# A kernel's work written as named jobs in one list, and its PSUM handed out as four pairs of banks from one queue

## The chip, the core and the metric

The kernel runs on one core of a Trainium2 chip. A core has a matrix engine (TensorE, PE in the profile, with its weight loads shown apart as PEld), a vector engine (VectorE, DVE), an engine for activations and copies (ScalarE, ACT), a general engine (GpSimd, POOL), and a queue engine that issues DMA transfers (SyncE, SP). Each runs its own instructions in program order and waits on semaphores for the others. Matmul results go to PSUM, which the kernel uses as eight banks of 512 fp32 numbers per partition; ScalarE or VectorE must copy a result out ("evict" it) before its banks can be written again.

The metric is the device time in microseconds. Before the change it is 213.2 us, the median of three runs (213.05 to 213.38).

## The reference

Two independent computations on sequences of length S = 2048 and width D = 576 in bf16, whose results stand side by side in the output.

```python
# A: 32 heads of width 18; every position attends to 8 positions at distance 0, 2, ..., 14
qkv = (x @ wqkv) -> q, k, v
logits = einsum("bhsd,bhswd->bhsw", q, kg) * scale     # kg: k at s - 2w, masked below 0
attn = softmax(logits)
a = einsum("bhsw,bhswd->bhsd", attn, vg) @ wo
# B: a 4-tap filter over k, times v, then a long convolution by FFT
k_shift = sum over t of k_pad[:, t:t+S] * shift_k[:, 3-t]
kv = k_shift * v
y = irfft(rfft(kv, 2S) * rfft(ssm_k, 2S))[:S] + kv * ssm_D
b = q * y
out = concatenate([a, b], -1)
```

## The kernel before

**Part A.** `project` makes q, k and v: for each block of 128 output columns and half of the sequence, a `unit` of eight to ten 512-wide matmuls fills a pair of banks (L363, L367, and the rest of the contraction in `tails`, L374, L380), and ScalarE evicts 1024 columns (L397). `logits` multiplies q by shifted k on VectorE (`product`, L822, into one of two halves of the tile `av`, or, for every third one while v's space there is still unused, into the tile `v`), and `total` sums over the head's columns with matmuls (L837) into one pair per five products; ScalarE evicts to `av` (L842). `softmax` runs on VectorE (L865 to L869, L882) and ScalarE (L871, L878, L879), with the sum over the eight positions on TensorE (L877). `spread` copies weights by DMA, `weigh` multiplies by v on VectorE (L947) and sums on TensorE (L964, L978), and `output` is the last projection (L1012, L1020), evicted by ScalarE (L1031).

**Part B.** `taps` computes kv in four blocks on VectorE (L560, L564, L580). `mirror` folds a block with matmuls into two pairs (L589, evicted by L592). `fold_filter` does the same with a block of the long filter (L650 into two pairs, L653), followed by three accumulating DMAs from POOL (L655, L657, L658). `filter_spectrum` transforms the filter (L610 and L611, evicted by L670), `x_spectrum` transforms kv (L766, L768). VectorE multiplies the spectra (L1098), TensorE adds the products (`sum_of`, L1126, two pairs held for a group, evicted by L1139), `inverse` transforms back (L1158, L1177, evicted by L1161, L1179; L1185 and L1199, evicted by L1206) and VectorE multiplies by q (L1212, L1167) before the store.

**What sets the order.** The scheduling of the framework is off (`manual_schedule`): instructions run in the order in which the Python code emits them. TensorE's fill-in work is collected as tuples in the list `units`; `until` emits the next few at each step of the main line, as many as the tuple `PLACES` says, and `need(label)` emits until none with that label is left. Further tuples (`FKS`, `FXS`, `EARLY`, `AT`) place single kinds, and a small model of the engines' clocks (`clk`, `pe`, `dve`) decides which unit comes first in some places and when late work (`tasks`) is due.

**PSUM.** The pool `pp` has two tags, "A" and "B", with two buffers each; every buffer is a pair of banks:

```python
pp = ctx.enter_context(tc.tile_pool(name="pp", bufs=2, space=PSUM))
def bank2(name, tag):
    return pp.tile([128, 2, 512], FP32, name=name, tag=tag)
```

A new tile of a tag takes the buffer of the tile two before it on that tag, and its first matmul waits until that one has been read. "A" serves projections, the filter folds (`ps_rev`, two at once), tables, outputs and the inverse; "B" serves the first transposes, mirrors (two at once), logits, softmax sums, weighted sums and the sums of products (two held). Filter and kv spectra alternate by `filler_tag`: filter units take "A" alone until the logits begin and then A, A, B in turn, kv units A and B.

Of the kernel before, what the change touches and what calls it, by code (L numbers as in the profile page):

```python
# [18 lines left out]
PLACES = (  # L19
    15, 4, 11, 2, 1, 0, 3, 4, 6, 4, 13, 4, 4, 0, 4, 3, 4, 2, 1, 3, 4, 3, 5, 5, 0, 7, 2, 2, 2, 1, 2, 2, 2, 2, 3,  # L20
    1, 0, 3, 2, 0, 8, 3, 0, 1, 12, 1, 1, 0,
)

FKS = (
    3, 1, 0, 0, 0, 0, 0, 0, 0, 0, 0, 0, 0, 0, 0, 0, 0, 0, 1, 0, 0, 0, 0, 2, 0, 0, 2, 0, 0, 0,
)
FXS = (
    7, 2, 0, 12, 13, 2, 0, 0, 4,
)

EARLY = (
    0, 0, 4,
)

AT = (
    2, 10, 17,
)
# [8 lines left out]
def kernel(  # L46
# [48 lines left out]
    pp = ctx.enter_context(tc.tile_pool(name="pp", bufs=2, space=PSUM))  # L95

    turns = {"fk": 0, "fx": 0, "wo": 0}

    def filler_tag(kind, tags):

        turns[kind] += 1
        return tags[turns[kind] % len(tags)]

    def bank2(name, tag):
        return pp.tile([128, 2, 512], FP32, name=name, tag=tag)

# [45 lines left out]
    warm = sp1.tile([128, 1], FP32, name="warm")  # L152
# [7 lines left out]
    def idle_work(n):  # L160
        ps = bank2("ps_idle", "A")
        for _ in range(n):
            nc.tensor.matmul(ps[:, 0, :], zeros[:, 0:128], zeros, start=True, stop=True)

# [137 lines left out]
    v = None  # L302
# [3 lines left out]

    units = deque()
    tasks = deque()
    clk = {"D": 0.0, "P": 0.0, "A": 0.0}
    psum = {"A": deque([0.0, 0.0]), "B": deque([0.0, 0.0])}  # L310

    def dve(n, fn, ready=0.0, ns=0.53):

        fn()
        clk["D"] = max(clk["D"], ready) + n * ns / 1000 + 0.125
        return clk["D"]

    def pe(us, tag, evac, ready=0.0, first=True, last=True):

        clk["P"] = max(clk["P"], ready, psum[tag].popleft() if first else 0.0) + us  # L320
        clk["A"] = max(clk["A"], clk["P"] + 0.1) + evac
        if last:
            psum[tag].append(clk["A"])
        return clk["A"]

    def pop(n=0):
        f = units[n][1]
        del units[n]
        f()

    places = iter(PLACES)

    def until():

        for _ in range(next(places, 0)):
            if units:
                p = max(clk["P"], psum["A"][0] if psum["A"] else 0.0)
                pop(next((n for n, u in enumerate(units) if len(u) < 4 or u[3] <= p), 0))

    def need(label):  # L340
        while any(u[2] == label for u in units):
            pop()

    def due(slack=0.0):

        while tasks and tasks[0][0] <= clk["D"] + slack:
            tasks.popleft()[1]()
# [4 lines left out]
    def dest(comp, ct):  # L352
        if comp == 0:
            return q, (ct * S if ct < 4 else 4 * S), 0
        return (k if comp == 1 else v), (ct * KW if ct < 4 else 4 * KW), PAD


    def project(comp, jj):
# [24 lines left out]
        def unit(ct, jj, jp, first, box):  # L383
            t, o, pad = dest(comp, ct)
            if jp == 0:
                box["ps"] = bank2("ps_proj", "A")
                if first:
                    tails(box["ps"], ct, jj, True)
            ps = box["ps"]
            body(ps, ct, jj, jp, first)  # L390
            if jp == 0:
                clk["P"] += 1.15 if first else 0.9
                return
            if not first:
                tails(ps, ct, jj, False)
            pe(0.9 if first else 1.15, "A", 1.02)
            nc.scalar.activation(view(t, o + pad + 1024 * jj, [[512, 2], [1, 512]]), ps[:], ACT.Copy)  # L397
            if ct == 4 and comp > 0:
                (nc.gpsimd if comp == 1 else nc.sync).dma_start(view(t, o, [[1, PAD]])[64:128, :], view(t, o + 1024, [[1, PAD]])[0:64, :])

        for ct in range(4) if jj < 2 else [4]:
            first = ct % 2 == 1 if ct < 4 else comp == 1
            box = {}
            for jp in range(2):
                units.append((0.9 + 0.25 * (jp != first), partial(unit, ct, jj % 2, jp, first, box),
                              f"v{jj}{ct}" if comp == 2 else f"proj{comp}"))
# [25 lines left out]
    def table_i(s):  # L432

        ps = bank2("ps_ti", "A")
# [27 lines left out]
    def pair_x():  # L462
        return pp.tile([128, 2, 1024], BF16, name="ps_x", tag="B")

    def early(f, us):
        f()
        clk["P"] += us

    def transpose_tail(jj):
        pt = pp.tile([128, 512], FP32, name="ps_x", tag="B")  # L470
# [4 lines left out]
        nc.scalar.activation(x5(jj), pt[:], ACT.Copy)  # L475

    def project_first(jp, ct0):

        ps = bank2("ps_proj", "A")
# [7 lines left out]
        nc.scalar.activation(view(q, S * ct0 + 512 * jp, [[S, 2], [1, 512]]), ps[:], ACT.Copy)  # L487

    def spread_taps(n0):
        n = min(256, D - n0)  # L490
        ps = bank2("ps_sk", "A" if n == 256 else "B")
        for h in range(0, n, 128):
            w = min(128, n - h)
            sk = skrow[:, 4 * (n0 + h):4 * (n0 + h + w)].rearrange("p (d j) -> p d j", j=4)
            for r in range(2):
# [4 lines left out]
                             ps[:].rearrange("p b (d j) -> p j (b d)", j=4)[:, :, 0:n], ACT.Copy)  # L500

# [3 lines left out]
    pts = [pair_x() for _ in range(2)]  # L505
# [6 lines left out]
    copy_tail(0, pts[1])  # L512
    spread_taps(256)
    sines += [table_x(0), table_x(1)]
    project_first(0, 0)
    pts = [pair_x() for _ in range(2)]
# [5 lines left out]
    copy_tail(1, pts[0])  # L522
    project_first(0, 2)
# [4 lines left out]
    for jj in range(2):  # L528
        if jj:
            project(0, jj)  # L530
        project(1, jj)
        if jj == 0:
            units.append((0.43, partial(early, partial(transpose_tail, 1), 0.43), "x"))
    project(0, 2)
    project(1, 2)

    def with_sine(f, n):
        f()
        sines[n]()
        if n == 1:  # L540
            nc.gpsimd.memset(TK[0:1, 0, 1, :], 0.5)
            for gi, sg in enumerate((1, -1, -1, 1)):
                nc.gpsimd.memset(TK[0:1, 0, 0, 128 * gi:128 * gi + 128], sg * 0.5)

    for n in range(2):
        units.insert(4 + 4 * n, (0.85, partial(early, partial(table_i, n), 0.85), "x"))
    for n, u in zip((1,), (1,)):
        units[n] = units[n][:1] + (partial(with_sine, units[n][1], u),) + units[n][2:]
    clk.update(D=0.0, P=2.0, A=0.0)
    psum["A"] = deque([0.0, 0.0])  # L550

    def taps(i):
# [4 lines left out]
        def mult(to, row, n):  # L559
            dve(2304 * n, lambda: nc.vector.tensor_tensor(  # L560
                to, view(kj, row * D, [[D, n], [D, 4], [1, D]]), view(skb, row * D, [[D, n], [0, 4], [1, D]]), ALU.mult))

        def add(o):
            dve(2304, lambda: nc.vector.tensor_tensor(kv, kv if o else pair[0], o or pair[1], ALU.add))  # L564
# [15 lines left out]
        return dve(2304, lambda: nc.vector.tensor_tensor(kv, kv, vt[:], ALU.mult))  # L580

    def mirror(i, n):

        kv = kv_of(i)
        pss = [bank2("ps_fold", "B") for _ in range(2)]
# [5 lines left out]
        for pm in range(2):  # L591
            nc.scalar.activation(halves(kv[:, 2 * n + pm, :]), pss[pm][:, :, 0:HD], ACT.Copy)  # L592
            pe(0.25, "B", 0.65)

# [14 lines left out]

    logits_run = [False]
# [20 lines left out]
    def negate(*ms):  # L634
        for m in ms:
            dve(288, lambda: nc.vector.tensor_scalar(minus_of(m), spare[m] if m < 2 else row(m, 0), -0.5 * ROOT, None, ALU.mult))

    def fold_filter(m):
        kt, swapped = kTok(m), m < 2

        def unit():
            minus = minus_of(m)
            pss = [bank2("ps_rev", "A") for _ in range(2)]
            for c in range(2):
                turns = [((flip2r, flip1)[c] if swapped else flip0, 1 - c), ((identn0, identn)[c], 2 + c)]
                if not swapped:
                    turns.insert(1, ((corner2, corner)[c], c))
                for n, (w, of) in enumerate(turns):
                    for h in range(2):
                        nc.tensor.matmul(pss[c][:, h, 0:HD], w[:], kt[:, of, HD * h:HD * h + HD], start=(n == 0),  # L650
                                         stop=(n == len(turns) - 1))
            for c in range(2):
                nc.scalar.activation(halves(kt[:, c, :]), pss[c][:, :, 0:HD], ACT.Copy, scale=0.5)  # L653
                pe(0.5, "A", 0.65)
            nc.gpsimd.dma_start(view(Ks, k_at(m, 2) + 2 * D, [[1, 2 * D]]), view(Ks, k_at(m, 2), [[1, 2 * D]]),  # L655
                                accum_op=ALU.add, max_dma_last_dim=2 * D)
            nc.gpsimd.dma_start(other(m)[1:128], kt[1:128, 0, :], accum_op=ALU.add)  # L657
            nc.gpsimd.dma_start(other(m)[0:1], minus, accum_op=ALU.add)  # L658

        return (1.0, unit, f"fold{m}")  # L660

    def filter_spectrum(m):
        def unit(gi, cs):
# [640 lines left out]
```

## Time and profile before

| | |
|---|---|
| timed runs | 213.2 us median (213.05, 213.2, 213.38) |
| profiled execution, from the first to the last instruction | 211.5 us |
| granted TensorE clock, mean over the span | 0.998 |
| ScalarE's idle time that a matmul ended, largest group (L968, `ps_acc`) | 8.3 us |
| evictions of filter spectra (L670) | 32, 688 ns each |
| evictions of kv spectra (L768) | 32, 673 ns each |
| logits products (L822), 4096 columns, into `av` | 12, 2283 ns each |

The profile is one execution. A group row gives the line, engine, operation, tiles (out<-in), shapes and count, then busy time and the mean of one, then the idle time of the engine just before, and what ended it. A wait row gives who waited for whom, the total, the number of times and the longest. A timeline row gives start and duration in microseconds, and in brackets the idle time before it and who ended it. A busy matmul row includes the time in which its result drains, so rows of successive matmuls overlap, and a short stop is only partly seen as idle time.

### The profile page before, as it was taken

How to read it: one execution, taken by the hardware profiler on the slowest of the kernel's cores; microseconds unless marked ns; L12 is line 12 of the kernel's file. 1: busy time of each engine (PE TensorE's matmuls, PEld its weight loads, DVE VectorE, ACT ScalarE, POOL GpSimd, SP SyncE). 2: the span in 40 equal slices, each digit the busy share in tenths (PEclk: the TensorE clock that was granted, in tenths of full speed). 3: DMA queues.
4: the chain of work that ended last, by engine and by line, in shares of the span. 5: the costliest groups of instructions: out<-in, count | busy, mean ns of one | idle time of the engine just before them, and what ended most of it. 6: DMA issues, size and time to landing. Idle time of an engine off the chain costs nothing.

```text
span 211.5 us, 5096 instructions
## 1 busy us (share of the span) xinstructions
PE 200.9 (95%) x2122; PEld 112.5 (53%) x2122; DVE 197.3 (93%) x150; ACT 151.0 (71%) x218; POOL 69.3 (33%) x104
## 2 busy tenths in 40 slices
PE   7999899999879999999999999999999999999891
PEld 2543344445545556563345566765567667676560
DVE  7989999999978999979979999999999999899982
ACT  3799766967797989984378688864487896765640
POOL 8999991023391367220090000004240000202000
PEclk9999999999999999999999999999999999999999
DMA  6999999999092636998999896589993105453034
GB/s 204 297 317 239 248 323 322 183 238 286 8 135 33 87 56 105 187 159 187 226 222 228 141 232 154 103 211 249 209 278 107 60 3 160 123 167 115 3 106 117
DMA packets 34084, 36.12 MB, mean 171 GB/s; under 512 B 17459, under 2 KB 28847, under 8 KB 34062
## 3 DMA queue, kind: packets, MB, share of 16 engines
q1 hardware_dynamic: 26380, 23.11, 43.8%
q0 software_dynamic: 5216, 10.19, 24.8%
q10 hardware_dynamic: 2466, 2.51, 3.6%
q8 instruction: 16, 0.26, 0.5%
q14 instruction: 6, 0.05, 0.1%
HBM read 13.11 MB, written 4.72 MB: 84 GB/s over the span
## 4 chain that ended last, share of the span: by engine, by line
PE 78%; ACT 10%; issue 3%; SPq 2%; DVE 2%; DMA 2%; DVEq 0%; ACTq 0%
PE ps_proj L363 13%; PE ps_z L1126 9%; PE ps_wo L1020 8%; PE ps_acc L964 7%; PE ps_inv L1158 7%; PE ps_fx L766 7%; PE ps_log L837 4%; PE ps_proj L483 4%; PE ps_fk L610 3%; ACT Ks L670 3%; PE ps_proj L374 2%; DMA Ks<-Ks 2%; SPq L212 2%; PE ps_rev L650 1%; PE ps_sk L496 1%
## 5 line engine op out<-in xcount | busy, mean ns | idle before, releaser
L363 PE MATMUL ps_proj<-xw 128*128 128x512 bf16 x160 | 37.5, 380 | 0.5 <-ACT qk L397 0.5
L822 DVE TENSOR_TENSOR av<-qk 128x4096 bf16<-128x4096 bf16 (+1 forms) x16 | 31.5, 2017 | 1.9 <-ACT xw L592 1.9
L363 PEld LDWEIGHTS <-xw 128*128 128x128 bf16 x160 | 14.4, 98 | 20.1 <-issue 4.8
L1139 ACT ACTIVATE av<-ps_z 128x768 bf16<-128x768 f32 x23 | 17.5, 811 | 5.6 <-PE ps_z L1126 5.6
L768 ACT ACTIVATE xw<-ps_fx 128x576 bf16<-128x576 f32 x32 | 18.8, 673 | 2.4 <-PE ps_fx L766 2.4
L397 ACT ACTIVATE qk<-ps_proj 128x1024 bf16<-128x1024 f32 x14 | 14.3, 1025 | 8.3 <-PE ps_proj L374 4.7
L670 ACT ACTIVATE Ks<-ps_fk 128x576 bf16<-128x576 f32 x32 | 19.0, 688 | 1.1 <-PE ps_fk L611 1.0
L1098 DVE TENSOR_TENSOR qk<-xw,Ks 128x2304 bf16<-128x2304 bf16 x14 | 18.6, 1355 | 1.0 <-PE ps_z L1126 0.7
L560 DVE TENSOR_TENSOR tB<-kj,skb 128x4608 bf16<-128x4608 bf16 (+1 forms) x8 | 19.3, 2416 | 0.1
L766 PE MATMUL ps_fx<-xw,TB 128*128 128x288 bf16 x128 | 17.9, 286 | 0.8 <-ACT xw L592 0.7
L1020 PE MATMUL ps_wo<-qk 128*128 128x288 bf16 x128 | 17.9, 287 | 0.0
L610 PE MATMUL ps_fk<-Ks,TB 128*128 128x384 bf16 x62 | 16.4, 326 | 1.2 <-ACT Ks L670 0.9
L1158 PE MATMUL ps_inv<-av,TI 128*128 128x288 bf16 (+1 forms) x112 | 15.6, 292 | 0.6 <-ACT av L1139 0.6
L766 PEld LDWEIGHTS <-TB 128*128 128x128 bf16 x128 | 12.0, 98 | 6.7 <-issue 3.5
L964 PE MATMUL ps_acc<-av,ident 64*64 64x512 bf16 x160 | 15.3, 379 | 0.0
L611 PE MATMUL ps_fk<-Ks,TB 128*128 128x192 bf16 x62 | 15.2, 246 | 0.0
L1087 POOL DMA_DIRECT2D TB<-in_B_q_dram x4 | 3.0, 738 | 36.7 <-DVE v L1098 23.5
L397 ACT ACTIVATE v<-ps_proj 128x1024 bf16<-128x1024 f32 x9 | 9.3, 1043 | 7.8 <-PE ps_proj L363 4.3
L1020 PEld LDWEIGHTS <-qk 128*128 128x128 bf16 x128 | 11.5, 98 | 6.2 <-issue 3.6
L968 ACT ACTIVATE qk<-ps_acc 128x1024 bf16<-128x1024 f32 x8 | 8.2, 1025 | 8.3 <-PE ps_acc L964 8.3
L947 DVE TENSOR_TENSOR av<-Ks,v 128x4096 bf16<-128x4096 bf16 x6 | 13.6, 2285 | 0.1
L1158 PEld LDWEIGHTS <-TI 128*128 128x128 bf16 x112 | 10.5, 98 | 5.6 <-issue 2.7
(194 smaller groups left out, 465.7 us busy)
## 6 DMA issues: line engine op xcount, KB each, us to landing
Ks<-Ks POOLq DMA_DIRECT2D x7, 576.0 KB, 8.3
TB<-av SPq DMA_DIRECT2D x12, 256.0 KB, 4.9
kj<-in_B_k_dram SPq DMA_DIRECT2D x6, 504.0 KB, 6.1
vt<-in_B_v_dram SPq DMA_DIRECT2D x8, 288.0 KB, 5.0
Ks<-av SPq DMA_DIRECT2D x8, 256.0 KB, 6.0
out_dram<-qk ACTq DMA_DIRECT2D x5, 288.0 KB, 3.2
Ks<-in_A_x_dram SPq DMA_DIRECT2D x2, 576.0 KB, 5.2
xw<-in_A_wqkv_dram SPq DMA_DIRECT2D x2, 576.0 KB, 6.0
```

What stands on the lines that cost most here:

```text
L363: nc.tensor.matmul(ps[:, jp, :], wq(kb, comp, 128 * ct, 128), xT(kb, 1024 * jj + 512 * jp, 512), **se)
L397: nc.scalar.activation(view(t, o + pad + 1024 * jj, [[512, 2], [1, 512]]), ps[:], ACT.Copy)
L560: dve(2304 * n, lambda: nc.vector.tensor_tensor(to, view(kj, row * D, [[D, n], [D, 4], [1, D]]), view(skb, row * D, [[D, n], [0, 4], [1, D ...
L610: nc.tensor.matmul(o[:, 0:2], w, rhs[:, 0:2], start=start, stop=stop)
L670: nc.scalar.activation(view(Ks, k_at(m, cs ^ (m & 1)) + 96 * gi, [[768, 3], [384, 2], [1, 96]]), acc3(ps), ACT.Copy, scale=(PSG, MSG)[cs][ ...
L766: nc.tensor.matmul(ps[:, pm, 0:HD], TX[:, 2 * pm + c, 128 * gi:128 * gi + 128], kv[:, 2 * c + pm, HD * h:HD * h + HD], start=(c == 0), sto ...
L768: nc.scalar.activation(view(xw, HB * XG[i] + 96 * gi + 1152 * h, [[HB, 2], [384, 3], [1, 96]]), view(ps, 0, [[512, 2], [96, 3], [1, 96]]), ...
L822: return P, at, step, dve(1024 * nj, lambda: nc.vector.tensor_tensor(view(P, at, [[step, 4], [256, nj], [1, 256]]), view(t, o + 256 * hh, ...
L964: nc.tensor.matmul(acc[64 * o:64 * o + 64, h, :], ident[64 * h:64 * h + 64, 64 * h:64 * h + 64], view(P, 256 * u, [[2048, 2], [1, 256]])[6 ...
L1020: nc.tensor.matmul(ps[:, r, 0:HD], oT(hh, j + 2 * r, t)[:, o:o + 128], wo[:, t // 2, t % 2, HD * h:HD * h + HD], start=(t == 0 and h == 0) ...
L1126: nc.tensor.matmul(view(acc[r], 512 * h, [[192, 2], [96, 2], [1, 96]])[o:o + 64], w[64 * h:64 * h + 64, 64 * h:64 * h + 64], pr[64 * h:64 ...
L1158: nc.tensor.matmul(ps[:, c, 0:n], TI[:, sl, pm, 128 * c:128 * c + 128], Yall[:, j % 2, pm, sl, c0:c0 + n], start=(pm == 0 and sl == 0), st ...
```

## The change

All scheduling machinery goes: `units`, `tasks`, `clk`, `until`, `need`, the placing tuples. Each piece of work becomes a function that is registered under a name (`job("x000", x_unit, 0, 0, 0)`), and one string lists the names in the order in which they are emitted. A name with a quote mark runs its small matmuls first.

```diff
+ORDER = """
+    T0 k00a k00b S1 k01a' k01b I0 k02a k02b k03a' I1 k03b X5 q10a q10b q11a' q11b Lk2 Lv2 T1 q12a q12b M00 q13a'
+    Lk3 Lv3 Lf3 Lf2 Lf1 Lf0 Lw Lo3 Lo2 Lo1 Lo0 Fr Ex T2 q13b k10a k10b M10 k11a' k11b k12a k12b M01 k13a' k13b
+    T3 N3 N2 M11 q24a q24b M20 k24a' k24b M21 F3 F2 M30 K310 K311 K312 K313 M31 SV Z2 x000 L000 L001 G000 G001
+    L002 N1 N0 L003 x001 x010 F1 G002 G003 L004 L010 x011 K300 K301 K302 G004 G010 L011 L012 K303 K210 K211 K212
...
+for name in ORDER.split():
+    jobs.pop(name.rstrip("'"))(*([True] if name[-1] == "'" else []))
+assert not jobs and len(slots) == 4
```

The names, as far as they are used below: T taps, k/q/v projections (a and b its two halves), I tables, M mirrors, F filter folds, K filter spectrum units, x kv spectrum units, L logits products, G logits sums, N the small negations (L636 before), p products of spectra, z their sums, i and b the inverse, g the gates.

The homes of products, which were computed by counters, become the tuples `LHOMES`, `VHOMES`, `OHOMES` and `PHOMES`.

PSUM becomes four tags of one buffer each. A queue holds the numbers of the free pairs; a tile takes the one at the head, and the job that emits its last eviction puts it back at the end, directly behind that eviction in the code.

```diff
-    pp = ctx.enter_context(tc.tile_pool(name="pp", bufs=2, space=PSUM))
-    def bank2(name, tag):
-        return pp.tile([128, 2, 512], FP32, name=name, tag=tag)
+    pp = ctx.enter_context(tc.tile_pool(name="pp", bufs=1, space=PSUM))
+    slots = deque(range(4))
+    def banks(name, dtype=FP32):
+        n = slots.popleft()
+        return pp.tile([128, 2, 2048 // (4 if dtype == FP32 else 2)], dtype, name=name, tag=f"p{n}"), n
...
-            tag = filler_tag("fx", "AB")
-            ps = bank2("ps_fx", tag)
+        ps, slot = banks("ps_fx")
...
             nc.scalar.activation(view(xw, HB * XG[i] + 96 * gi + 1152 * h, [[HB, 2], [384, 3], [1, 96]]),
                                  view(ps, 0, [[512, 2], [96, 3], [1, 96]]), ACT.Copy)
-            pe(0.52, tag, 0.65)
+        slots.append(slot)
...
     def mirror(i, n):
-        pss = [bank2("ps_fold", "B") for _ in range(2)]
+        pss, held = zip(*[banks("ps_fold") for _ in range(2)])
...
+        slots.extend(held)
```

The two gates that read PSUM directly on VectorE (`gate_last`) give their pairs back when they are emitted. One SBUF tile of four bytes a partition changes its pool, which puts the tiles allocated after it 32 bytes further on:

```diff
-    warm = sp1.tile([128, 1], FP32, name="warm")
+    warm = main.tile([128, 1], FP32, name="warm")
```

More of the change, by code (lines that the diff above doesn't have):

```diff
@@ L301 @@
     q, k = qk[:, 0:4 * S + 1024], qk[:, 4 * S + 1024:]
[L302 to L347, printed above, removed]
+    late = {}
     def halves(ap):
@@ L522 @@
     copy_tail(1, pts[0])
+    slots.extend(held)
     project_first(0, 2)
@@ L632, in minus_of, with negate @@
         return (view(Ks, k_at(1, 0) + D * (1 + m), [[1, D]]) if m else view(xw, 11 * HB + 2 * D, [[1, D]]))[0:1]
[L634 to L636 removed]
+    def negate(m):
+        nc.vector.tensor_scalar(minus_of(m), spare[m] if m < 2 else row(m, 0), -0.5 * ROOT, None, ALU.mult)
     def fold_filter(m):
         kt, swapped = kTok(m), m < 2
[L641 to L660, printed above, removed]
```

846 lines of the change are left out of this document (366 added, 480 removed).

## The prediction

> **What bounds the kernel now.** I read the page's totals and chain first, then the waits of TensorE and of VectorE, then the timelines of the one stretch to which the largest waits lead.
>
> ```profile
> span 211.5 us, 5096 instructions
> PE 200.9 (95%) x2122; PEld 112.5 (53%) x2122; DVE 197.3 (93%) x150; ACT 151.0 (71%) x218; POOL 69.3 (33%) x104
> ...
> PE 78%; ACT 10%; issue 3%; SPq 2%; DVE 2%; DMA 2%; DVEq 0%; ACTq 0%
> ```
>
> TensorE and VectorE are both busy nearly throughout, and 78% of the chain that ended last is TensorE. Ten per cent of it is ScalarE: TensorE stood behind evictions there. Since two engines are almost full, an edit that leaves every duration alone can only win what both of them lose in waiting.
>
> ```profile
> PE ps_fk L610 <- ACT Ks L670: 0.9, 2, 0.7
> PE ps_fx L766 <- ACT xw L592: 0.7, 1, 0.7
> PE ps_rev L650 <- ACT Ks L653: 0.7, 1, 0.7
> ...
> PE ps_proj L363 <- ACT qk L397: 0.5, 1, 0.5
> ...
> PE ps_wo L1012 <- ACT v L1206: 0.3, 1, 0.3
> ```
>
> These rows (engine and line that waited, who ended it, us in total, times, longest) are the waits of TensorE that an eviction ended and that are waits for a bank, not for data: the matmul reads nothing that the named copy wrote. They are 3.1 us of idle time, and the loss is larger, as a matmul's row outlasts its slot in the stream (below).
>
> ```profile
> DVE av L822 <- ACT xw L592: 1.9, 1, 1.9
> DVE av L882 <- ACT av L879: 1.3, 1, 1.3
> DVE av L947 <- PE ps_log L837: 1.1, 1, 1.1
> ```
>
> VectorE, the other full engine, loses its largest piece once, 1.9 us, before a product of L822. That wait decides what TensorE's savings are worth: ahead of it VectorE runs on data that TensorE does not make (taps, then products), so a faster TensorE alone moves nothing.
>
> ```profile
> 55.09 4.47 DVE L822 TENSOR_TENSOR av<-qk 128x4096 bf16<-128x4096 bf16 x2
> 59.50 2.27 DVE L822 TENSOR_TENSOR v<-qk 128x4096 bf16<-128x4096 bf16 x1
> ...
> 61.92 0.29 DVE L636 TENSOR_SCALAR xw<-Ks 1x576 bf16<-1x576 bf16 x1
> 64.06 3.43 DVE L822 TENSOR_TENSOR av<-qk 128x4096 bf16<-128x4096 bf16 x2 [1.85 <-ACT xw L592]
> ```
>
> Start, duration, instruction, idle before it. The product at 64.06 writes the half of `av` that the first product (55.09) filled, so it may start when the first logits sum (L837, eight matmuls) has read that half. The row names the copy L592, but that copy only let the sum start. TensorE on the same stretch:
>
> ```profile
> 55.06 0.41 PE L650 MATMUL ps_rev<-Ks,identn 128*128 128x288 bf16 x2
> 56.16 0.41 PE L650 MATMUL ps_rev<-Ks,flip 128*128 128x288 bf16 x2 [0.68 <-ACT Ks L653]
> ...
> 57.72 0.68 PE L589 MATMUL ps_fold<-xw,fold 128*64 128x288 bf16 x8
> 58.33 0.34 PE L610 MATMUL ps_fk<-Ks,TB 128*128 128x384 bf16 x1
> 58.50 0.25 PE L611 MATMUL ps_fk<-Ks,TB 128*128 128x192 bf16 x1
> ...
> 59.24 0.25 PE L611 MATMUL ps_fk<-Ks,TB 128*128 128x192 bf16 x1
> 60.22 0.32 PE L610 MATMUL ps_fk<-Ks,TB 128*128 128x384 bf16 x1 [0.74 <-ACT Ks L670]
> ...
> 61.34 0.68 PE L589 MATMUL ps_fold<-xw,fold 128*64 128x288 bf16 x8
> 62.76 0.65 PE L766 MATMUL ps_fx<-xw,TB 128*128 128x288 bf16 x4 [0.74 <-ACT xw L592]
> 63.34 1.05 PE L837 MATMUL ps_log<-av,E 128*32 128x512 bf16 x16
> ```
>
> Three bank waits stand in the 8 us ahead of that sum. Tag "A" has two pairs: the filter folds take both at once and the filter units turn them over, while tag "B" stands idle or belongs to the mirrors.
>
> **The change part by part.** *Order.* The built programs have the same instructions in the same order on all five engines, so nothing is moved past anything. What differs is the bank pair of each PSUM tile, hence what 129 instructions, all on TensorE, wait for.
>
> *Why the new waits come no later.* All evictions but a handful (first transposes, last block) run on ScalarE in program order, and the queue hands out the pair whose release was written first. With four pairs the n-th tile has to wait for some release as late as the (n-4)-th under any rule; the queue waits for exactly that one. Single tiles do wait for later releases than before (the mirrors at 57.72 and 61.34 had their own pairs), but a TensorE instruction ahead of them waited for a later one still. Behind them queue the filter units, L766 and the logits sum, and VectorE's product waits for that sum; the sums below carry this.
>
> *Four stalls ahead of the sum*, each measured from where the stream would go on.
>
> (a) Table transposes to projection:
>
> ```profile
> 22.81 0.64 PE L438 MATMUL ps_ti<-ident,TB 128*64 128x128 bf16 x16
> 22.92 1.03 ACT L397 ACTIVATE qk<-ps_proj 128x1024 bf16<-128x1024 f32 x1
> 24.00 0.81 PE L363 MATMUL ps_proj<-xw 128*128 128x512 bf16 x3 [0.55 <-ACT qk L397]
> ```
>
> The transposes end at 23.45; the projection sits 0.55 idle for the copy that ends at 23.95. It will take a pair freed four tiles back, long done, so 0.55 goes, and about 0.06 by which matmuls that follow unhindered overlap: 0.6. VectorE is untouched; TensorE and ScalarE run 0.6 early to the next stall.
>
> (b) 56.16: the row before ends at 55.47, and rows that follow unhindered overlap by 0.17 (58.33 + 0.34 against 58.50), so 55.30 was possible: 0.86. The second fold will use the pairs of the mirror before it, whose copies are the next row's; a first copy of two takes 0.65 (L766 at 62.76 waited for the one of 62.06 and came 0.70 after it, 0.05 of that the signal), so the one of 54.37 is there at 55.0, less 0.6: 54.4. Nothing is left of the wait: TensorE is 1.46 early.
>
> ```profile
> 54.37 1.19 ACT L592 ACTIVATE xw<-ps_fold 128x576 bf16<-128x576 f32 x2
> 55.43 1.22 ACT L653 ACTIVATE Ks<-ps_rev 128x576 bf16<-128x576 f32 x2
> 57.33 1.19 ACT L653 ACTIVATE Ks<-ps_rev 128x576 bf16<-128x576 f32 x2 [0.68 <-PE ps_rev L650]
> 58.43 1.20 ACT L592 ACTIVATE xw<-ps_fold 128x576 bf16<-128x576 f32 x2
> 59.51 1.20 ACT L670 ACTIVATE Ks<-ps_fk 128x576 bf16<-128x576 f32 x2
> 60.91 1.20 ACT L670 ACTIVATE Ks<-ps_fk 128x576 bf16<-128x576 f32 x2 [0.19 <-PE ps_fk L611]
> 62.06 1.19 ACT L592 ACTIVATE xw<-ps_fold 128x576 bf16<-128x576 f32 x2
> ```
>
> (c) 60.22: the unit ahead ends at 59.49 and would overlap by 0.17, so 59.32: 0.90. It waited for the first copy of 59.51 and will wait for the first of 58.43, two earlier. ScalarE itself: its 0.68 idle at 57.33 shrinks, since it is free at 56.65 less 0.6, so this row starts near 56.1, 1.24 early; the copy of 58.43 then ends at 58.43 + 0.65 - 1.24 = 57.84, and the unit starts at 57.9: 2.3 early.
>
> (d) 62.76: a mirror is followed after 0.61 (57.72 to 58.33), so 61.95: 0.81. It waited for the first copy of 62.06 (62.71), and will wait for the first of 60.91. That copy is 1.4 early (ScalarE again back to back), so ends at 60.2; L766 starts at 60.25: 2.5 early.
>
> *What VectorE makes of it.* The logits sum ends 2.5 early, about 61.4 in place of 63.9, ahead of the small L636 pair that ends at 62.21. The product starts at 62.25, not 64.06: **1.8 us**, with 0.8 us of TensorE's lead in hand.
>
> *After that.* TensorE, ScalarE and VectorE are all at least 1.8 early, loads from HBM are long landed, and the rest of the program can only shift with them. Two more pieces: VectorE's 1.3 us wait (L882) is ended by copies behind TensorE and ScalarE, which lead by up to 0.7 more: 0 to 0.5, I take 0.2, being nearer to VectorE's own pace (28.56 of 30 us busy in the window below). Bank waits of the second half (L1012 0.3) fall where VectorE's products come last: 0 to 0.3, I take 0.
>
> ```profile
> 50.00:66.00 16.00, 13.85 (x134) 8.34 (x131) 14.04 (x12) 12.75 (x22) 8.38 (x11) 1.00 0.59 110
> 66.00:96.00 30.00, 29.50 (x276) 17.27 (x274) 28.56 (x20) 26.49 (x44) 12.80 (x10) 1.00 0.67 109
> ```
>
> (Window, length, busy us of PE, PEld, DVE, ACT, POOL, granted clock, DMA share, GB/s.)
>
> *Costs.* Thirteen data waits move from a matmul to its weight load, which then cannot run ahead. A load takes
>
> ```profile
> L1126 PEld LDWEIGHTS <-ident 64*64 64x64 bf16 x240 | 7.1, 107 | 2.9 <-DVE v L1098 0.6 <-issue 0.2
> ```
>
> 107 ns (the first figure after the bar is us in total, the second ns of one), so 0 to 1.4 us. I take 0: it costs only where TensorE waits for VectorE, and there VectorE sets the pace; without that cover it is 0.1 a place. Four more separate waits stand in TensorE's stream, 0 to 0.1 each by the same row; 0 taken, hidden in TensorE's lead. `warm` moves from one pool to another, and the tiles after it lie 32 bytes further; L822's products into `av` and into `v`, two differently placed tiles, take 2.24 (4.47 for two) and 2.27 us above, so 0.
>
> *Sum*, against the profiled execution: 211.5 - 1.8 - 0.2 + 0 = 209.5. The timed median, 213.2, is 1.7 above this span, and I keep that: **211.2 us**.
>
> **The rivals.**
>
> *ScalarE sets the pace (0.22).* For it: 26.49 of 30 us busy in the second window, and the 1.9 us row names its copy. If the product follows ScalarE, it gains that engine's shift of 1.4, and if TensorE's further lead is lost in the wait at L882, down to 0.6. Against: the product reads nothing of L592, and 0.8 us of slack is left. 211.7 to 212.6.
>
> *The gain is given back (0.07).* VectorE's next waits, 1.3 and 1.1 us, grow by what was won, because the sums that end them hang on another thing, a DMA of the filter folding or a product. Against: both rows name work on engines that lead. Within 0.4 of 213.2.
>
> *The clock falls (0.06), slower.* Place: 56 to 64, where pairs now turn over without a stop. The start of the trace shows the price: four 512-wide matmuls
>
> ```profile
> 1.27 1.89 PE L163 MATMUL ps_idle<-xw 128*128 128x512 bf16 x4 [1.27 <-DVE pib L148]
> 18.61 1.90 PE L363 MATMUL ps_proj<-xw 128*128 128x512 bf16 x8
> ```
>
> take 1.89 us, where later eight take 1.90: 0.24 us lost a matmul. It decides from about nine such matmuls (2.0 / 0.24); two stretches of 4 us at half pace cost 2 each: 213.2 - 2.0 + 4 = 215.2. Against: both windows above stand at clock 1.00, with the stops in them, and the change removes stops. The Trainium skill has the rule behind this rival ("TensorE: Matmul & The Clock Gate", section "A second HAM failure mode: psum-queue depth-cycling"): rotating matmul groups through banks makes many short idles between which the clock drops and recovers. This kernel already rotates, and its trace shows no drop; by the rule the time would be the 215.2 above.
>
> *More (0.04).* All of L882's slack and the second half's waits count: 211.2 - 0.5 - 0.3 = 210.4.
>
> **How the numbers follow.** The forecast has 0.61, with its own range 210.7 to 211.7; the rivals 0.22, 0.07, 0.06 and 0.04. A measurement of this kernel tells 0.2% (0.4 us) from no change. Faster: 0.61 + 0.22 + 0.04 = 0.87; same 0.07; slower 0.06. The range 210.4 to 212.6 holds forecast, ScalarE's case and most of the unknown costs (1.4 on top of 211.2), and leaves out some 0.15.
>
> **What would show it.** Right: TensorE's rows for L610, L766, L650 and L363 lose their waits for ScalarE; the product that stood at 64.06 starts near 62.3 with under 0.1 idle; VectorE's wait at L882 is no longer than 1.3; durations per group and the granted clock stay. Wrong: a new VectorE wait of 1 us or more between 64 and 110; the L882 wait growing by as much as L822's shrank; a clock under 1.00 between 55 and 65; or matmul spacing behind the moved weight-load waits growing where VectorE waits for TensorE.

## The result and the profile after

The changed kernel takes 210.3 us (median of four runs, 209.65 to 210.63); four runs of the kernel before, beside it, have a median of 213.29 us (213.05 to 213.43). The ratio is 0.986, with a 95% interval of 0.984 to 0.988. The forecast was 211.2 us, its range 210.4 to 212.6: the direction and the main mechanism came as foretold, but the gain is 3.0 us in place of 2.0, and the time is just outside the range.

The page of the changed kernel, its totals and the engines' shares of the chain that ended last:

```profile
span 208.9 us, 5092 instructions
PE 200.0 (96%) x2114; PEld 111.5 (53%) x2122; DVE 197.2 (94%) x150; ACT 150.5 (72%) x218; POOL 69.7 (33%) x104
...
PE 78%; DVE 10%; issue 5%; ACT 4%; DVEq 0%
```

The span fell by 2.6 us. No engine's busy time moved by more than 1.0 us, so the gain is idle time. ScalarE's share of the chain went from 10% to 4%, and VectorE's rose from 2% to 10%: TensorE stands behind copies less. Its waits (engine and line that waited, who ended it, us in total, times, longest):

```profile
PE ps_idle L161 <- DVE pib L146: 1.3, 1, 1.3
PE ps_proj L320 <- issue: 0.6, 4, 0.2
PE ps_inv L999 <- ACT av L977: 0.6, 1, 0.6
PE ps_log L714 <- DVE av L700: 0.4, 2, 0.3
PE ps_inv L1018 <- ACT av L977: 0.3, 1, 0.3
PE ps_acc L833 <- DVE av L808: 0.2, 1, 0.2
PE ps_back L1027 <- ACT v L1020: 0.2, 1, 0.2
PE ps_z L964 <- DVE qk L945: 0.2, 1, 0.2
```

The first row is the start of the kernel and was the same before. The four short stops by "issue" are rows that the trace lacks: it has 153 matmuls of L320 for the 160 of L363 before, and e5_warm_back below, with the same pairs, has 160 and no such stop. Each of the others names something that the matmul reads. All the bank waits shown of before (3.1 us) are gone, and so is a sixth row (L610 for a logits copy, 0.24 us, below). (Lines have moved: L822 is now L700, L882 L750, L947 L808, L837 L714, L766 L676, L610 L563, L650 L598, L670 L614, L592 L544, L397 L353.) VectorE's waits:

```profile
DVE av L808 <- PE ps_log L714: 1.1, 1, 1.1
...
DVE xw L513 <- DMA kj<-in_B_k_dram: 0.9, 1, 0.9
DVE av L975 <- PE ps_z L964: 0.9, 1, 0.9
DVE TB L1009 <- PE ps_back L1027: 0.8, 1, 0.8
DVE qk L945 <- PE ps_z L964: 0.7, 1, 0.7
DVE av L750 <- ACT av L758: 0.6, 1, 0.6
```

The 1.9 us wait at the logits product has no row any more, and the 1.3 us wait at the scaling by the softmax sum has become 0.6. The two places in VectorE's timeline, a later product by v, and the logits sum in TensorE's (start, duration, instruction, idle before it):

```profile
62.14 0.29 DVE L586 TENSOR_SCALAR xw<-Ks 1x576 bf16<-1x576 bf16 x1
62.36 3.41 DVE L700 TENSOR_TENSOR av<-qk 128x4096 bf16<-128x4096 bf16 x2
...
91.38 1.23 DVE L750 TENSOR_TENSOR av<-av 128x2048 bf16<-128x2048 bf16 x1 [0.62 <-ACT av L758]
...
130.71 2.29 DVE L808 TENSOR_TENSOR av<-Ks,v 128x4096 bf16<-128x4096 bf16 x1
```

```profile
60.30 0.65 PE L676 MATMUL ps_fx<-xw,TB 128*128 128x288 bf16 x4
60.88 1.05 PE L714 MATMUL ps_log<-av,E 128*32 128x512 bf16 x16
```

The last two of VectorE's in the kernel before:

```profile
93.74 1.23 DVE L882 TENSOR_TENSOR av<-av 128x2048 bf16<-128x2048 bf16 x1 [1.30 <-ACT av L879]
...
133.30 2.29 DVE L947 TENSOR_TENSOR av<-Ks,v 128x4096 bf16<-128x4096 bf16 x1
```

Against it, the sum starts at 60.88 in place of 63.34, and the product at 62.36 in place of 64.06, 1.70 us early. The scaling is 2.36 early. The product by v, which had 0.15 us of idle time ahead of it before, is 2.59 early, and from there to the end the difference stays. So the span's 2.6 are 1.70 + 0.66 + 0.23.

### The profile page after: what moved, and what is told of

It is laid out like the page before. It is cut to its first block, busy times and chain, and to the rows that moved or that the text cites. A ratio compares the mean times of both kernels' runs of the same rounds, so it can differ in the third digit from the quotient of the medians.

```text
span 208.9 us, 5092 instructions
## 1 busy us (share of the span) xinstructions
PE 200.0 (96%) x2114; PEld 111.5 (53%) x2122; DVE 197.2 (94%) x150; ACT 150.5 (72%) x218; POOL 69.7 (33%) x104
## 4 chain that ended last, share of the span: by engine, by line
PE 78%; DVE 10%; issue 5%; ACT 4%; DVEq 0%
PE ps_proj L320 16%; PE ps_wo L883 7%; PE ps_acc L819 6%; PE ps_z L964 6%; PE ps_fx L676 6%; PE ps_inv L999 5%; PE ps_fk L563 4%; PE ps_proj L435 3%; PE ps_log L714 3%; PE ps_proj L331 3%; PE ps_proj L324 3%; DVE qk L945 2%; DVE av L700 2%; PE ps_fk L564 2%; PE ps_fold L541 2%
## 5 line engine op out<-in xcount | busy, mean ns | idle before, releaser
L320 PE MATMUL ps_proj<-xw 128*128 128x512 bf16 x153 | 36.2, 380 | 0.7 <-issue 0.6
L700 DVE TENSOR_TENSOR av<-qk 128x4096 bf16<-128x4096 bf16 (+1 forms) x16 | 31.4, 2012 | 0.0
L320 PEld LDWEIGHTS <-xw 128*128 128x128 bf16 x160 | 14.3, 98 | 19.5 <-issue 4.3
L678 ACT ACTIVATE xw<-ps_fx 128x576 bf16<-128x576 f32 x32 | 18.9, 676 | 1.8 <-PE ps_fx L676 1.6
L353 ACT ACTIVATE qk<-ps_proj 128x1024 bf16<-128x1024 f32 x14 | 14.3, 1023 | 7.7 <-PE ps_proj L331 4.1
L614 ACT ACTIVATE Ks<-ps_fk 128x576 bf16<-128x576 f32 x32 | 18.9, 718 | 0.8 <-PE ps_fk L564 0.6
L676 PE MATMUL ps_fx<-xw,TB 128*128 128x288 bf16 x128 | 17.8, 286 | 0.1
L563 PE MATMUL ps_fk<-Ks,TB 128*128 128x384 bf16 x62 | 16.2, 326 | 0.0
L676 PEld LDWEIGHTS <-TB 128*128 128x128 bf16 x128 | 12.0, 98 | 5.9 <-issue 2.5
L353 ACT ACTIVATE v<-ps_proj 128x1024 bf16<-128x1024 f32 x9 | 9.2, 1039 | 7.8 <-PE ps_proj L320 4.3
L822 ACT ACTIVATE qk<-ps_acc 128x1024 bf16<-128x1024 f32 x8 | 8.2, 1023 | 8.0 <-PE ps_acc L819 8.0
L808 DVE TENSOR_TENSOR av<-Ks,v 128x4096 bf16<-128x4096 bf16 x6 | 13.7, 2287 | 0.0
L622 POOL DMA_DIRECT2D Ks<-Ks x7 | 11.1, 2100 | 7.1 <-ACT Ks L614 6.6
```

Source lines behind the costliest of these rows:

```text
L320: nc.tensor.matmul(ps[:, jp, :], wq(kb, comp, 128 * ct, 128), xT(kb, 1024 * jj + 512 * jp, 512), **se)
L563: nc.tensor.matmul(o[:, 0:2], w, rhs[:, 0:2], start=start, stop=stop)
L614: nc.scalar.activation(view(Ks, k_at(m, cs ^ (m & 1)) + 96 * gi, [[768, 3], [384, 2], [1, 96]]), acc3(ps), ACT.Copy, scale=(PSG, MSG)[cs][ ...
L676: nc.tensor.matmul(ps[:, pm, 0:HD], TX[:, 2 * pm + c, 128 * gi:128 * gi + 128], kv[:, 2 * c + pm, HD * h:HD * h + HD], start=(c == 0), sto ...
L700: tt(view(P, at, [[step, 4], [256, nj], [1, 256]]), view(t, o + 256 * hh, [[0, 4], [512, nj], [1, 256]]), view(tk, ok + 2 + 8 * ug + 256 * ...
```

## The experiments

Twelve kernels ran, in three groups, each group beside the kernel before on one chip (medians 213.11, 213.12 and 213.13 us). Where a line number belongs to an experiment it is that kernel's own.

| kernel | us | ratio to before, 95% |
|---|---|---|
| e1_old_pairs | 213.12 | 1.0013 (0.9995 to 1.0031) |
| e2_queue_first | 210.77 | 0.9886 (0.9872 to 0.9899) |
| e3_queue_mid | 212.45 | 0.9970 (0.9958 to 0.9983) |
| e4_queue_late | 212.97 | 0.9987 (0.9976 to 0.9997) |
| e5_warm_back | 210.23 | 0.9865 (0.9849 to 0.9881) |
| e6_sum_early | 210.06 | 0.9853 (0.9836 to 0.9871) |
| e7_logits_early | 210.34 | 0.9872 (0.9852 to 0.9891) |
| e9_keys_first | 210.76 | 0.9886 (0.9870 to 0.9903) |
| e10_old_keys_first | 214.52 | 1.0079 (1.0050 to 1.0109) |
| e14_early_matmuls | 210.35 | 0.9871 (0.9853 to 0.9890) |
| e15_late_matmuls | 210.59 | 0.9882 (0.9865 to 0.9899) |
| e16_late_max | 210.69 | 0.9884 (0.9867 to 0.9902) |

### The list with the old pairs (e1_old_pairs)

The queue stays in the code, but the pair that a tile gets is read from a table of the old ones.

```diff
+PAIRS = (
+    0, 2, 1, 3, 2, 0, 1, 2, 3, 0, 1, 0, 1, 0, 1, 0, 1, 0, 3, 0, 1, 0, 2, 3, 1, 0, 2, 3, 1, 0, 2, 3, 1, 2, 3, 0, 2, 3, 1, 2,
...
     slots = deque(range(4))
+    pairs = iter(PAIRS)
...
-        n = slots.popleft()
+        slots.popleft()
+        n = next(pairs)
```

> The job list of the changed kernel, with the 200 PSUM tiles given the same pairs of banks as in the kernel before, so every wait is the old one. Theory A (the pairs make the whole gain): the time of before, 213.3 us, within 0.4; VectorE waits about 1.85 us ahead of the product that follows the first logits sum and 1.3 us ahead of the scaling by the softmax sum. Theory B (writing the work as jobs, or the moved 32-byte tile, gives part of it, such as the 0.4 us of the gain that lies outside the span): 212.9 us or less, with both waits unchanged.

213.12 us, no difference from before. VectorE's timeline has the stall back:

```profile
64.14 2.29 DVE L711 TENSOR_TENSOR av<-qk 128x4096 bf16<-128x4096 bf16 x1 [2.08 <-ACT xw L555]
```

Writing the work as a list, and moving `warm`, gave nothing; the pairs made all of the gain. Theory B falls.

### The queue in one stage at a time (e2_queue_first, e3_queue_mid, e4_queue_late)

The same edit with three other tables. Each has the queue's pairs in one stage and the old ones elsewhere; together the stages hold the 129 changed waits once.

> The queue's pairs for the first 55 PSUM tiles, up to the first logits sum of half 0, and the old pairs after that; 44 of the 129 waits change. Theory A (the prediction's step, only sized too small): the 1.85 us wait ahead of the product after the first logits sum goes, the 1.3 us wait ahead of the scaling stays within 0.2, time 211.2 to 211.5 us. Theory C (the second wait shortens because the first stage hands ScalarE a lead, so that the first 55 tiles carry nearly everything): the second wait falls to about 0.6, time 210.4 to 210.7 us.

> Old pairs for the first 55 tiles, the queue's for the next 42 (to the softmax sum of half 0), old after; 26 waits change. Theory A (the two stages are separate, each shortening its own wait): the 1.85 us wait stays, the 1.3 us wait falls to about 0.6, time 212.5 to 212.8 us. Theory C (the middle tiles matter only once the first stall is gone): the 1.3 us wait stays above 1.1 with the 1.85 us wait still there, time 213.0 to 213.4 us.

> Old pairs up to the softmax sum of half 0 (97 tiles), the queue's for the other 103; 59 waits change. Theory A by the prediction's step (second half gains 0 to 0.3): 213.0 to 213.4 us, both early waits unchanged, VectorE waits of 0.7 to 1.2 us in the second half as before. Theory D (the last 103 tiles make the 0.6 us that the measured gain has over what the two early waits explain): 212.6 to 212.8 us.

The first stage alone takes 2.34 us off, the middle one 0.66, the last one 0.14: 3.1 together, where the whole change takes 3.0. The stages add up. The first is larger than theory A had it (210.77 for 211.2 to 211.5) without being theory C, whose 0.6 us wait did not come. VectorE in e2_queue_first:

```profile
61.96 3.41 DVE L711 TENSOR_TENSOR av<-qk 128x4096 bf16<-128x4096 bf16 x2
...
91.41 1.22 DVE L761 TENSOR_TENSOR av<-av 128x2048 bf16<-128x2048 bf16 x1 [1.06 <-ACT av L769]
```

The product is 2.10 us early here, since VectorE itself came earlier in this execution, and the wait at the scaling shrinks by 0.24 (1.30 to 1.06). That 0.24 is what TensorE's lead is worth there. (In e5_warm_back below, which has the queue's pairs everywhere, VectorE comes as early, its product starts at 61.91, and this wait is 0.64; so the early arrival does not make the 1.06.) In e3_queue_mid the product stands at 64.06 as before, and the scaling still starts 0.59 early, as theory A had it (the time is just under its range):

```profile
93.15 1.22 DVE L761 TENSOR_TENSOR av<-av 128x2048 bf16<-128x2048 bf16 x1 [0.66 <-ACT av L769]
```

So the wait for the softmax sum has a cause in its own stage. It is seen in ScalarE's timeline, first of the kernel before:

```profile
70.20 1.06 ACT L842 ACTIVATE av<-ps_log 128x1024 bf16<-128x1024 f32 x1
71.11 0.70 ACT L670 ACTIVATE Ks<-ps_fk 128x576 bf16<-128x576 f32 x1
72.00 2.28 ACT L670 ACTIVATE Ks<-ps_fk 128x576 bf16<-128x576 f32 x4 [0.19 <-PE ps_fk L611]
```

and then of e3_queue_mid:

```profile
70.20 1.06 ACT L729 ACTIVATE av<-ps_log 128x1024 bf16<-128x1024 f32 x1
71.10 2.87 ACT L625 ACTIVATE Ks<-ps_fk 128x576 bf16<-128x576 f32 x5
```

Before, TensorE stood at 71.32 for a bank that a logits copy held,

```profile
71.32 0.32 PE L610 MATMUL ps_fk<-Ks,TB 128*128 128x384 bf16 x1 [0.24 <-ACT av L842]
...
83.40 0.32 PE L610 MATMUL ps_fk<-Ks,TB 128*128 128x384 bf16 x1 [0.17 <-ACT Ks L670]
```

so the unit came late to ScalarE. From the copy at 72.00 on ScalarE is 0.31 to 0.35 early in e3_queue_mid, up to 89 us; two pauses on the way (0.62 and 0.18 before) are as long in both kernels. The stop at 83.40 changes nothing in ScalarE's rows. The rest of the 0.59 comes at the last copies ahead of the softmax sum, before and then in e3_queue_mid:

```profile
89.20 1.21 ACT L397 ACTIVATE v<-ps_proj 128x1024 bf16<-128x1024 f32 x1
90.53 2.28 ACT L670 ACTIVATE Ks<-ps_fk 128x576 bf16<-128x576 f32 x4
92.88 0.39 ACT L878 ACTIVATE av<-ps_tot 128x256 f32<-128x256 f32 x1
```

```profile
88.87 1.21 ACT L364 ACTIVATE v<-ps_proj 128x1024 bf16<-128x1024 f32 x1
89.77 2.48 ACT L625 ACTIVATE Ks<-ps_fk 128x576 bf16<-128x576 f32 x4
92.29 0.38 ACT L768 ACTIVATE av<-ps_tot 128x256 f32<-128x256 f32 x1
```

Before, the filter copy starts 1.33 behind the projection copy, in e3_queue_mid 0.90. TensorE starts the unit for it at 89.83 before and at 89.00 in e3_queue_mid, so ScalarE no longer has to wait for it. Both parts reach VectorE undiminished: ScalarE's 0.59 at the sum is the 0.59 of the scaling. Which of the 26 changed waits made TensorE 0.83 early there was not tried one by one.

In e4_queue_late both early waits stand (1.6 and 1.2 us). Of the last stage's gain the trace shows 0.24 at 133.30, where the product's 0.15 of idle time goes. The timed 0.14 is nearer to the prediction's step there than to theory D, but its interval (0.06 to 0.51 us) shuts neither out.

### `warm` back in its pool (e5_warm_back)

```diff
-    warm = main.tile([128, 1], FP32, name="warm")
+    warm = sp1.tile([128, 1], FP32, name="warm")
```

> The changed kernel with the one-element tile `warm` put back into the pool of the first stage, so that only the shift of addresses by 32 bytes is undone. Theory A (the pairs make the whole gain): the changed kernel's time, 210.3 us within 0.5, all waits as there. Theory B (the shift has a part in it): 210.9 us or more.

210.23 us: the shift of addresses costs nothing. This kernel also shows what differs from one execution to the next. VectorE's first product of the keys, here and (second) in the changed kernel:

```profile
11.71 1.36 DVE L513 TENSOR_TENSOR xw<-kj,skb 128x2304 bf16<-128x2304 bf16 x1 [0.57 <-DMA kj<-in_B_k_dram]
...
61.91 2.27 DVE L700 TENSOR_TENSOR av<-qk 128x4096 bf16<-128x4096 bf16 x1
```

```profile
12.08 1.36 DVE L513 TENSOR_TENSOR xw<-kj,skb 128x2304 bf16<-128x2304 bf16 x1 [0.94 <-DMA kj<-in_B_k_dram]
```

Keys that land 0.37 us earlier, and a logits product that starts 0.45 earlier (61.91 for 62.36) in a span that is 0.6 shorter (208.3 for 208.9). With the old pairs the keys were 0.36 earlier in e1_old_pairs than in the kernel before, and the product there started 0.08 later (64.14 for 64.06).

### Two moves in the list (e6_sum_early, e7_logits_early)

```diff
-    K101 K102 K103 U2 K010 x021 x030 K011 sm0b L101 K012 K013 v24a v24b G100 G101 L102 K000 K001 K002 K003 sm0c
+    K101 K102 K103 U2 K010 x021 x030 K011 sm0b L101 K012 K013 v24a v24b G100 G101 L102 K000 K001 sm0c K002 K003
```

> The changed kernel with the job sm0c (the softmax sum of half 0) moved ahead of the fold jobs K002 and K003 in the list. Theory A (VectorE's remaining 0.62 us wait at L750 is there because two fold jobs, 1.08 us on TensorE, and their copies on ScalarE stand ahead of the sum): the wait goes, VectorE runs on without a stop, 209.6 to 209.9 us. Rival (the time is taken back by ScalarE, which makes the two fold copies later, or by the logits job behind them): the wait goes but one of the same size appears before 105 us, 210.2 us or more.

```diff
-    v03a' v03b x200 x201 G113 G114 D1 D2 Wl U1 V04 v10a v10b A04 sm1a v11a' sm1b V10 V11 v11b v12a v12b sm1c
+    v03a' v03b G113 x200 x201 G114 D1 D2 Wl U1 V04 v10a v10b A04 sm1a v11a' sm1b V10 V11 v11b v12a v12b sm1c
```

> The changed kernel with the logits job G113 moved ahead of the two shift jobs x200 and x201, which take TensorE 1.1 us. Theory A (VectorE's 1.12 us wait at L808 is the wait for G113 to have read the buffer that the product writes over, and G113's operands are ready 1.1 us earlier): the wait falls to 0.2 or less, 209.2 to 209.5 us. Rival (VectorE waits for G114, the later of the two, whose operand VectorE finishes itself only at 103.7): the wait stays above 0.8, time within 0.3 of the changed kernel's.

Neither is told apart from the changed kernel (210.06 and 210.34 us, intervals that overlap its own). Each took the wait away that it aimed at, and got another: the rival's in the first kernel (though its time is just under the rival's 210.2), in the second one that neither theory had. VectorE in e6_sum_early, and then in e7_logits_early:

```profile
90.57 1.22 DVE L750 TENSOR_TENSOR av<-av 128x2048 bf16<-128x2048 bf16 x1
...
95.75 7.83 DVE L700 TENSOR_TENSOR av<-qk 128x4096 bf16<-128x4096 bf16 x4 [0.62 <-PE ps_log L714]
```

```profile
106.48 0.69 DVE L739 TENSOR_TENSOR xw<-av 128x1024 bf16<-128x1024 bf16 x1 [0.37 <-ACT av L718]
...
117.52 2.29 DVE L808 TENSOR_TENSOR av<-Ks,v 128x4096 bf16<-128x4096 bf16 x1 [0.56 <-PE ps_acc L819]
```

The sum's 0.62 comes back at 95.75, where a product waits for a logits sum to have read the buffer that it overwrites. In e7_logits_early the theory named the right job (the product starts 1.02 us early), and 0.37 + 0.56 of it return behind later sums. One wait less on one of the two full engines is not yet time where the next sum makes it wait again. No kernel tried here beats the changed one by more than its runs spread.

### A delay of TensorE, with either set of pairs (e9_keys_first, e10_old_keys_first)

The load of x's second quarter moves behind three transfers of keys; the second kernel has the same edit and the old pairs.

```diff
     load_w(nc.sync, 0)
-    load_x(1)
...
         for a, b in ((3, 7), (0, 3)) if i == 0 else ((0, 7),):
+            if i == 0 and a == 0:
+                load_x(1)
```

> The changed kernel with the load of the second quarter of x issued behind the first three transfers of the keys in place of ahead of them: the keys that VectorE waits for 0.94 us at L513 no longer stand behind 576 KB of x in the queue. Theory A (with the stall ahead of the first product gone, the head of VectorE's row reaches the end of the kernel, so what comes earlier at 12 us comes earlier at the end): wait at L513 0.2 or less, 209.4 to 209.8 us. Rival (the first stage has slack that TensorE, ScalarE or x sets, as it had before the change): the wait at L513 goes and a wait of the same size stands ahead of the first logits product, 210.2 us or more.

> The old pairs, as in e1_old_pairs, with the keys loaded ahead of the second quarter of x, as in e9_keys_first. With the queue's pairs that edit brought VectorE forward by 0.44 us at 55 us, and lost it again in a new wait of 0.45 us for ScalarE at the first logits product, that came from TensorE and ScalarE being later. Theory A (with the old pairs ScalarE's fold copies set the start of that product, so VectorE's earlier arrival is worth nothing, and what x costs TensorE is seen alone): the wait at that product 2.1 to 2.6 us, 213.1 to 213.6 us. Rival (TensorE's later start is swallowed by its stops for banks before the first product): the wait 1.9 to 2.2, 212.7 to 213.1.

With the queue the rival came (a new wait of 0.45 us, 210.76 us); with the old pairs the kernel is slower than either theory had it. x comes later than TensorE needs it (a wait of 1.36 us for x with the queue, 0.69 with the old pairs), and the logits sum is about a microsecond late in both. With the queue (e9_keys_first), TensorE and VectorE:

```profile
61.90 1.05 PE L715 MATMUL ps_log<-av,E 128*32 128x512 bf16 x16
```

```profile
62.63 3.43 DVE L701 TENSOR_TENSOR av<-qk 128x4096 bf16<-128x4096 bf16 x2 [0.45 <-ACT xw L545]
```

With the old pairs (e10_old_keys_first):

```profile
64.44 1.05 PE L726 MATMUL ps_log<-av,E 128*32 128x512 bf16 x16
```

```profile
65.17 2.29 DVE L712 TENSOR_TENSOR av<-qk 128x4096 bf16<-128x4096 bf16 x1 [3.11 <-ACT xw L556]
```

This pair of kernels separates the two regimes. With the old pairs a sum that is 1.03 late (63.41 in e1_old_pairs) makes the product 1.03 late (64.14 to 65.17), and the time 1.4 us longer. With the queue a sum that is 1.02 late (60.88) makes the product 0.27 late (62.36): the other 0.75 us is the lead that TensorE had in hand. Against e5_warm_back, where the keys landed early and the sum started at 60.48, the sum is 1.42 late and the product 0.72 (61.91), so the lead is 0.70 there. The time is 0.5 us longer. The waits name the fold copies L545 and L556, but both products start 0.73 us behind the sum, as the product of before did (64.06, 0.72 behind 63.34). From the named copy they start 1.02 us (61.61) and 2.01 us (63.16) away, and 2.00 before (62.06): they follow the sum, not the copy.

### More work for one engine (e14_early_matmuls, e15_late_matmuls, e16_late_max)

The first diff is e14_early_matmuls; e15_late_matmuls has (2, 2, 0, 0) in place of (1, 2, 1, 0). The second is e16_late_max.

```diff
+            if (comp, ct, jj, jp) == (1, 2, 1, 0):
+                for kb in range(4):
+                    nc.tensor.matmul(ps[:, jp, :], wq(kb, comp, 128 * ct, 128), xT(kb, 1024 * jj + 512 * jp, 512),
+                                     start=(kb == 0), stop=(kb == 3))
             for kb in range(4):
```

```diff
             tt(t4, at[:, 0:4, :], at[:, 4:8, :], ALU.max)
+            if hh == 1:
+                tt(t4, at[:, 0:4, :], at[:, 4:8, :], ALU.max)
```

> The changed kernel with four projection matmuls of 128x512 run twice at about 33 us (0.95 us more of TensorE, same result). Theory T (after the change TensorE sets the pace, 98.7% busy from 24 to 62 us, and the 0.8 us that the prediction left in hand is not there): 211.0 to 211.4 us, with a new wait of VectorE for ScalarE or TensorE ahead of the first logits product. Theory V (VectorE sets it, TensorE has 0.8 us in hand): 210.2 to 210.6 us, no new wait before 64.

> The changed kernel with four projection matmuls of 128x512 of the values run twice at about 98 us (0.95 us more of TensorE, same result). Theory T (from 92 us on TensorE sets the pace, so that waits taken from VectorE come back): 211.0 to 211.4 us. Theory V (VectorE sets it): 210.2 to 210.6 us.

> The changed kernel with VectorE's first maximum of half 1 (0.69 us, at 107 us) run twice, same result. Theory T (TensorE sets the pace from 92 us on, VectorE follows with waits of 0.7 to 1.1 us that can take it up): 210.2 to 210.5 us, VectorE's waits behind 107 us shorter by 0.4 us or more in sum. Theory V: 210.9 to 211.1 us, waits as they were.

The early matmuls stood at 42.35 us, not 33, and cost nothing: 210.35 us. Theory T falls for this stage, although TensorE is 98.7% busy in it in the changed kernel (window, length, busy us of PE, PEld, DVE, ACT, POOL, granted clock, DMA share, GB/s):

```profile
24.00:62.00 38.00, 37.51 (x287) 18.03 (x289) 37.48 (x24) 29.60 (x45) 17.16 (x32) 1.00 0.93 225
```

TensorE in e14_early_matmuls, and VectorE:

```profile
42.35 1.03 PE L319 MATMUL ps_proj<-xw 128*128 128x512 bf16 x4
...
61.34 1.05 PE L718 MATMUL ps_log<-av,E 128*32 128x512 bf16 x16
```

```profile
62.17 3.41 DVE L704 TENSOR_TENSOR av<-qk 128x4096 bf16<-128x4096 bf16 x2
```

The sum's start and 0.73 make 62.07, and VectorE gets there at 62.17 without a stop: 0.1 of the lead was left. The late ones, at 97.23, and the second maximum, at 107.45, cost some 0.3 and 0.4 us of their 0.95 and 0.69 by the medians. In e15_late_matmuls VectorE's wait at 104.83 absorbs much of it:

```profile
100.91 3.43 DVE L704 TENSOR_TENSOR av<-qk 128x4096 bf16<-128x4096 bf16 x2 [0.72 <-PE ps_log L718]
105.08 2.29 DVE L812 TENSOR_TENSOR av<-TB,v 128x4096 bf16<-128x4096 bf16 x1 [0.74 <-PE ps_log L718]
```

A new wait of 0.72, and the next one down from 1.12 to 0.74. The time of e15_late_matmuls lies at the end of theory V's range, that of e16_late_max between the two ranges, and both within the changed kernel's own spread (1.0 us in four runs), so the times decide little. The traces say more when they are counted from VectorE's first logits product (55.31 us in the changed kernel) to the start of its last instruction (204.57), which leaves out when the keys came. That stretch is 149.26 us in the changed kernel and 149.14 in e5_warm_back, 149.33 in e15_late_matmuls and 149.79 in e16_late_max. So TensorE's extra work costs 0.1 to 0.2 of its 0.95, VectorE's 0.5 to 0.65 of its 0.69, and VectorE's waits behind 107 us are only 0.15 shorter in sum. With one execution of each, that speaks for theory V: VectorE sets the pace there more than TensorE.

## Why the prediction was right or wrong

*Order and waits: right.* With the list and the old pairs the time is that of before, so the 129 waits on TensorE carry everything.

*The four stalls ahead of the logits sum: right.* All four are gone, and the sum starts 2.46 us early; the steps (a) to (d) had made it 2.5.

*The logits product, 1.8 us: right.* It started at 62.36 (62.25 forecast) with no idle time, 1.70 early in this execution and 2.10 in e2_queue_first. The spread is VectorE's own arrival, which the forecast had fixed at its time of before. "0.8 us of TensorE's lead in hand" measured 0.70 to 0.75 in e9_keys_first.

*The wait at L882, "0 to 0.5, I take 0.2": the step that failed.* It measured 0.66. The step asked only what was left of TensorE's lead when it came to that wait, and for that 0.2 was good (0.24 in e2_queue_first). It did not ask what the stage's own bank waits cost: the list of stalls ended with the first logits sum, and of the two stops behind it one (0.17 at 83.40) was inside a row of waits that the step did not open, and the other (0.24 at 71.32) was not among the rows shown. With the stage's own waits changed and nothing else, the scaling is 0.59 early in e3_queue_mid: 0.33 because the stop at 71.32 no longer holds ScalarE up, which nothing behind it takes up again, and 0.26 because TensorE, 0.83 early by 89 us, no longer lets ScalarE wait at the last copies. The upper bound was wrong for the same reason; lead and own stops make 0.24 + 0.59 = 0.83 when measured apart, 0.66 together.

*The second half, "0 to 0.3, I take 0": within its bounds, at the upper end.* It measured 0.23 in the trace, 0.14 in time in e4_queue_late.

*The sum.* 211.5 - 1.70 - 0.66 - 0.23 = 208.9, which is the span. *What lies around the span, 1.7: right.* The profiled execution took 210.57, 1.67 above its span. The median is another 0.27 lower; the profiled execution was one of the two slowest of the four, with keys that came late. So of the 0.9 us between forecast and median 0.46 are the step at L882, 0.23 the second half and 0.27 this execution, less the 0.1 by which the product gained less. By this sum 0.2 at L882 would have put the time inside the range.

*Costs taken as 0: right.* VectorE's waits for TensorE in the second half are 0.9, 0.8 and 0.7, as they were at the same lines before (L1137, L1167, L1098), so the moved waits cost nothing where they could; `warm` costs nothing (e5_warm_back). Durations per group stay, except the filter copies (L614), whose rows are longer in the mean (718 for 688 ns); the group's busy time is not (18.9 for 19.0 us), and the reason is open.

*The rivals.* ScalarE does not set the product's start: in e9_keys_first the product again follows the sum by 0.73, and the copy that its wait names by 1.02 in place of 2.00. The gain is not given back. The clock did not fall: it is 0.999, with 200 PSUM tiles going round through four pairs, the 512-wide projection matmuls (L320) keep their mean of 380 ns, and the rival's 215.2 did not come. Its price was read from the slow matmuls at 1.27 us; the granted clock is 1.00 there too (0 to 3.5 us of before), so that the clock made them slow is not shown. What the Trainium skill says of such rotation ("TensorE: Matmul & The Clock Gate", section "A second HAM failure mode: psum-queue depth-cycling"), that TensorE's short idles between groups make its clock swing, is not seen in this trace, whose mean is 0.999. "More", at 210.4, is the case that came; 0.04 was too little for it, since the bank waits behind the first logits sum all spoke for it.

## What to carry to other kernels

Where a pool change takes waits away, work out every stage's own stops up to the wait that it feeds, not only those ahead of the largest one; a short stop of a feeding engine counts in full when nothing behind it takes it up again before the point where the full engine waits (0.33 us here, over two pauses that stayed as long). Two tags that are each full at different times lose to one queue over all buffers when the releases come in program order: here 1.4%, by four pairs of banks that were there before. Once a stall ahead of the pace-setting engine is gone, what it had hidden is to be asked for next: with it a microsecond of TensorE's delay moved VectorE's product by a microsecond, without it the first 0.7 us moved nothing.

## What the runs showed of the hardware that had not been expected

The keys that VectorE waits for at 12 us land between 11.6 and 12.2 us in executions that have the same loads in the same order. With the old pairs the stall at 64 us swallowed this: in the four traces with them in the first stage the product starts at 64.06 to 64.14, whenever the keys came (11.60 to 12.19). With the queue it goes on: in the eight traces with its pairs there the product starts 50.19 to 50.29 us behind VectorE's first product of the keys (11.67 to 12.08). That it reaches the end is a reading of one pair of executions (0.37 earlier, span 0.6 shorter); the one attempt to load the keys earlier delayed x, and did not test it alone.

A busy share says little of slack: TensorE was 98.7% busy between 24 and 62 us, and 0.95 us more work there cost nothing that the times show (210.35 for 210.30 us).
